# A planner's allowance for transposing DMAs, and the order of loads and distances of attention that go with it

## The chip, the cores and the metric

The kernel runs on one core of a Trainium2 chip. The metric is the device time of one execution in microseconds (us). Names of engines in the profile: PE is TensorE's matrix product (PEld its weight load), DVE is VectorE, ACT is ScalarE, POOL is GpSimd, SP is SyncE, which here only issues DMAs. A transposing DMA copies a tile from SBUF to SBUF and swaps its axes on the way.

## The reference

Chunked attention with a memory, and behind it a gated feed-forward network (FFN) on the same rows:

```python
# q, k, v: (4, 8, 768, 64); mem_k, mem_v: (4, 8, 8, 64); chunk 32, 16 keys left, 8 right
for c in range(24):
    q_c   = q[:, :, 32*c : 32*c+32]
    k_ctx = k[:, :, max(0, 32*c-16) : min(768, 32*c+40)]      # v_ctx alike
    k_full, v_full = concat(mem_k, k_ctx), concat(mem_v, v_ctx)
    a = softmax(q_c @ k_full.T / 8)
    out[:, :, 32*c : 32*c+32] = a @ v_full
x = out.transpose(0, 2, 1, 3).reshape(3072, 512)
gate = maximum(x @ w_gate, 0)          # 512 x 1536
return (gate * (x @ w_val)) @ w_out    # 1536 x 512, float32
```

## The kernel before

**Tiles.** The 3072 rows are 24 attention tiles of 128 rows, `a` = 0 to 23, six to a batch. One tile goes through these steps: transpose queries and keys (`t`), put them where the scores read them (`tc`), scores (`s`, L297), row maximum, subtraction, exponential, sum, reciprocal, normalising (`max`, `sub`, `exp`, `sum`, `rec`, `nrm`), transpose of the normalised weights (`p`, then `pc` if it went through PSUM), product with the values (`v`, L363), copy to the FFN's input (`x`). The FFN works on blocks of 3, 3, 4, 4, 3, 3 and 4 tiles (`BLOCKS`). Block `blk` does twelve times: gate product, value product (`f`, L409), relu on ACT (`r`, L415), multiplication on DVE (`g`, L421). Then come the output products (`o`, L430; four groups of three to a tile), a copy out of PSUM on ACT (`oc`, L91, tile `o_sb`) and a store issued by SP (`os`, L440). `o_sb` has three buffers, the PSUM pool of the FFN (`fps`) has four.

**Who transposes.** Tiles 0 to 5 come as pairs, up to tile 13 (queries) or 14 (keys) tile by tile, and are transposed on PE. From there on (`BY_DMA`, `BY_DMA_P`) queries, keys and weights are transposed by DMAs that SP issues (`qk_dma` L271 with tiles `qT` and `k_t`, `p_dma` L350 with tile `pT`). Keys are then copied from `k_t` to their place by ACT (`tc`, L91 `kT<-k_t`).

**Loads.** POOL issues all loads of queries, keys, values and weights, in the order of the string `LOADS`: `Q0` and `K0` are pairs, `q10` and `k10` single tiles, `v13` a half of batch 0's values (half 1, head pair 3), `z` a memset, `w` a group of FFN columns, `o` a half of `w_out`, `m` the memory's values, `b2` the four loads of batch 2's values. Tiles of queries and keys share 16 buffers.

**Order.** Nothing reorders at run time: each engine runs its list in order. `schedule()` makes the lists by simulating the engines once, when the kernel is built. It gives every step a duration, keeps the time at which each result is there (`done`) and lets a free engine take the ready step with the lowest priority. `LEAD` sets, for each block, how many of the FFN's steps the attention of that block's tiles goes ahead. For a transposing DMA issued by SP (`key[0] in "tpx"`) `done` is the end of the issue plus `BESIDE`, 13 us, or plus `LANDING`, 3 us. Before the change `BESIDE` holds while loads are left to issue, or up to the time at which the queries of the last tile, `("qk", 23, 0)`, are there. In `LOADS` two entries stand behind that tile's `q23` load and others: the last are `k22` and `b3`.

Of the kernel before, what the change touches and what calls it, by code (L numbers as in the profile page):

```python
# [20 lines left out]
def kernel(  # L21
# [24 lines left out]
    NT = B * TPB  # L46
# [3 lines left out]
    CTX = 16 + CH + 8  # L50
    NSET = 2
    BLOCKS = [3, 3, 4, 4, 3, 3, 4]
    LEAD = [24, 10, -1, 2, 7, 6, 14, 22]
    LAST = ((0, 384), (384, 512))
    BY_DMA = (14, 15)
    BY_DMA_P = 14
    LANDING = 3.0
# [1 line left out]
    MEM_BY_SP = 0  # L59
    MEM_LEAD = (0,0,4,4)  # L60
    BY_DMA_X = 24
    BESIDE = 13.0
    LOADS = """Q0 K0 K1 i K2 Q1 Q2 v00 z0 v12 v03 v01 v02 w0 w1 v10 v13 v11 w2 k10
               k8 w3 q6 q7 k7 k6 w4 k9 z2 q9 q8 o1 z1 z3 o0 m b1 k11 q11 q16
               q10 k12 k14 k15 k23 q13 q12 q21 k16 k13 q14 k21 k20 q15 k19 b2 k18 q17 k17 q23
               q18 q22 q19 q20 k22 b3"""

    KEY_RUNS = ((CH, KW, 0), (0, CH, NMEM), (KW, 64, KW))
    assert sum(BLOCKS) == NT and NMEM == 8 and D == 64 and H == 8
# [378 lines left out]
    ops, loads = {}, []  # L448
# [41 lines left out]
    def pace(a):  # L490
        blk = block_of[a]
        if starts[blk] < TPB:
            return []
        m = NDC * (blk - 1) + NDC * (a - starts[blk]) // BLOCKS[blk] - LEAD[blk]
        return [("f", *divmod(max(m, 0), NDC), 0)]
# [4 lines left out]
    for a in range(NT):  # L500
        b, t = divmod(a, TPB)
# [139 lines left out]
    def load_by(name):  # L641
        what, n = name[0], int(name[1:] or 0)
        if what in "qk":
            load_qk_op(n, "qk".index(what))
        elif what in "QK":
            load_pair_op(n, "QK".index(what))
        elif what == "i":
            load("ident", 0, 0.55, lambda: make_identity(nc, ident_h))
        elif what == "v":
            load_v_half(n // 10, [n % 10])  # L650
        elif what == "w":
            load_w_op(n)
        elif what == "z":
            load_zero(n)
        elif what == "m":
            for par in range(2):
                load(("vm", par), 256, 0.3, lambda par=par: mem_values(par))
        elif what == "o":
            load(("wo", n), 768, 4.1, lambda n=n: load_out(n))
        elif what == "b":  # L660
            load_batch(n)

    for name in LOADS.split():
        load_by(name)

    def timed(d):
        return isinstance(d, tuple) and len(d) == 2 and isinstance(d[1], float)
# [8 lines left out]

    def schedule():
        done, started, times = {}, set(), [0.7, 1.25]
        locked = 0.0
        free = {e: 1.25 if e == "POOL" else 0.7 for e in ("PE", "ACT", "DVE", "SP", "POOL")}  # L680
        queue_end, flying, gives = 0.0, [], []
        todo = {e: [] for e in free}
        order, n_load = [], 0
        names = lambda o: [d[0] if timed(d) else d for d in o["deps"]] + o["after"]
        missing = {k: len(set(names(o))) for k, o in ops.items()}
        users = {}
        for k, o in ops.items():
            for d in set(names(o)):
                users.setdefault(d, []).append(k)

        def offer(k):
            for e in ops[k]["eng"]:
                bisect.insort(todo[e], (ops[k]["prio"], k), key=lambda x: x[0])

        for k in ops:
            if not missing[k]:
                offer(k)

        def ready(o, t, margin=0.0):
            if any(d not in started for d in o["after"]):  # L700
                return False
            for d in o["deps"]:
                d, lag = d if timed(d) else (d, 0.0)
                if d not in done or done[d] + lag + margin > t + 1e-9:
                    return False
            return all(room[r] >= o["take"].count(r) for r in o["take"])

        while len(started) < len(ops) + len(loads):
            t = heapq.heappop(times)
            while times and times[0] <= t + 1e-9:  # L710
                heapq.heappop(times)
            for g in [g for g in gives if g[0] <= t + 1e-9]:
                gives.remove(g)
                room[g[1]] += 1
            flying = [f for f in flying if f > t]
            moved = True
            while moved:
                moved = False
                for e in ("POOL", "PE", "ACT", "DVE", "SP"):
                    if free[e] > t + 1e-9:  # L720
                        continue
                    if e == "POOL":
                        if n_load == len(loads):
                            continue
                        o = loads[n_load]
                        if len(flying) >= 8 or not ready(o, t):
                            continue
                        n_load += 1
                        key = o["key"]
                        if o["n"]:  # L730
                            end = t + 0.62 + 0.27e-3 * o["n"]
                            queue_end = max(queue_end, end + 0.8) + o["work"]
                            flying.append(queue_end + 1.0)
                            done[key] = queue_end + (1.2 if n_load < 8 else 2.4 if n_load < 45 else 6.0 if key[0] == "vl" else 4.0)
                        else:
                            end = done[key] = t + o["work"]
                        if locked > t:
                            end += 0.25
                        fn = o["fn"]
                    else:  # L740
                        o = None
                        for _, key in todo[e]:
                            late_pe = e == "PE" and t > 36.0 and ops[key]["prio"][0] == 1
                            if ready(ops[key], t, MARGIN if late_pe else 0.0):
                                o = ops[key]
                                break
                        if o is None and e == "PE" and "ident" in done and 6.0 < t and ("f", 0, 0, 0) not in started:
                            order.append((t, idle_product))
                            free[e] = t + 0.1
                            heapq.heappush(times, free[e])  # L750
                            continue
                        if o is None:
                            continue
                        for x in o["eng"]:
                            todo[x].remove((o["prio"], key))
                        d = o["eng"][e] * (1.8 if e == "PE" and (t < 10.0 and key[0] == "t" or t < 24.0 and key[0] == "p") else 1.0)
                        if e == "DVE" and holds_port(key):
                            end = max(t + d, free["POOL"] + d - 0.1 if free["POOL"] > t else 0.0)
                            locked = end
                        else:  # L760
                            end = t + d
                        done[key] = end + (0.25 if e == "PE" else LAG)
                        if e == "SP" and key[0] in "tpx":
                            done[key] = end + (BESIDE if n_load < len(loads) or t < done["qk", NT - 1, 0] else LANDING)
                        if e == "SP" and key[0] in MOVE:
                            queue_end = max(queue_end, t) + MOVE[key[0]]
                        fn = lambda o=o, e=e: o["fn"](e)
                        for g in o["give"]:
                            g, lag = g if isinstance(g, tuple) else (g, 0.0)
                            gives.append((done[key] + lag, g))  # L770
                            heapq.heappush(times, done[key] + lag)
                    for r in o["take"]:
                        room[r] -= 1
                    started.add(key)
                    for k in users.get(key, ()):
                        missing[k] -= 1
                        if not missing[k]:
                            offer(k)
                    order.append((t, fn))
                    free[e] = end  # L780
                    for x in (end, done[key], done[key] + 0.2, done[key] + 1.5, done[key] + MARGIN):
                        heapq.heappush(times, x)
                    moved = True
            assert times, [k for k in ops if k not in started][:20]
        return order

    for _, fn in schedule():
        fn()
# [30 lines left out]
```

## Time and profile before

| what | value |
|---|---|
| runs | 241.6, 244.89, 245.3 us; median 244.89 us |
| the profiled execution | 243.38 us, of which the span of its instructions is 241.6 us |
| granted TensorE clock | 1.000 |
| busy PE, DVE, ACT, POOL | 225.4, 144.9, 114.9, 92.2 us |
| share of the chain that ended last | PE 60%, DMA 20%, POOL 13% |

The span runs from the first to the last instruction of the trace; the execution's time is 1.78 us longer. Times within the trace count from the span's start. A row of a timeline shows the start of a group of instructions, its length, and in brackets how long the engine had been idle and what ended that. A row of the chain shows start and length of a piece of the sequence of work that ended last. A row of waits shows the total, the number and the longest.

### The profile page before, as it was taken

The numbers are of one execution on the slowest core, as the hardware profiler recorded it, in microseconds if no ns is written. First come the engines' busy times: TensorE is split into PE (matmuls) and PEld (weight loads), VectorE is DVE, ScalarE is ACT, GpSimd is POOL, SyncE is SP. The second block draws the span as 40 slices with busy tenths as digits, with TensorE's granted clock in tenths as the row PEclk, the third lists the DMA queues.
The fourth block names the chain that finished last, engine by engine and source line by source line (L and its number), as shares of the span: only waits on it lengthen the run. The fifth ranks groups of instructions, "written<-read, shape, count | busy, mean of one in ns | idle before, by whom it ended". The sixth has DMA issues, their size and how long they took to land.

```text
span 241.6 us, 5912 instructions
## 1 busy us (share of the span) xinstructions
PE 225.4 (93%) x2446; PEld 125.0 (52%) x2446; DVE 144.9 (60%) x259; ACT 114.9 (48%) x248; POOL 92.2 (38%) x106
## 2 busy tenths in 40 slices
PE   0797989999999999998989799999999999999994
PEld 0676655665544645544434354455556664444442
DVE  4599944569999099775968665059973440234300
ACT  3785753446533855663255452257465441232212
POOL 8999998898648792425700000000000000000000
PEclk9999999999999999999999999999999999999999
DMA  6999999999999999999999962510333001200022
GB/s 72 166 129 137 158 150 175 186 180 175 147 165 207 205 176 96 131 141 120 130 223 163 150 91 27 171 43 3 69 87 111 1 3 43 88 0 0 3 87 87
DMA packets 121115, 27.17 MB, mean 112 GB/s; under 512 B 111232, under 2 KB 118144, under 8 KB 121088
## 3 DMA queue, kind: packets, MB, share of 16 engines
q0 software_dynamic: 101344, 16.61, 95.4%
q1 hardware_dynamic: 19744, 10.18, 21.4%
q8 instruction: 19, 0.31, 0.5%
q14 instruction: 8, 0.07, 0.1%
HBM read 33.24 MB, written 6.29 MB: 164 GB/s over the span
## 4 chain that ended last, share of the span: by engine, by line
PE 60%; DMA 20%; POOL 13%; issue 2%; SPq 2%; DVE 1%; ACT 0%; ACTq 0%; POOLq 0%
PE out_ps L430 19%; PE v_ps L409 19%; PE g_ps L409 18%; DMA qk_b<-in_k_dram 9%; POOL v_bd L187 7%; DMA qk_b<-in_q_dram 4%; DMA pT<-p_n 3%; DMA out_dram<-o_sb 3%; POOL qk_p L218 3%; DMA w_gate_sb<-in_moe_w_gate_dram 2%; SPq L271 2%; PE xT_ps L363 2%; POOL w_gate_sb L118 1%; POOL w_val_sb L118 1%; PE s_ps L297 1%
## 5 line engine op out<-in xcount | busy, mean ns | idle before, releaser
L421 DVE TENSOR_TENSOR gvT<-v_ps,g_relu 128x384 f16<-128x384 f32 (+1 forms) x84 | 51.4, 612 | 57.9 <-PE v_ps L409 47.5
L409 PE MATMUL v_ps<-xT,w_val_sb 128*128 128x384 f16 (+1 forms) x336 | 75.9, 349 | 0.6 <-ACT o_sb L91 0.6
L409 PE MATMUL g_ps<-xT,w_gate_sb 128*128 128x384 f16 (+1 forms) x336 | 75.9, 349 | 0.3 <-DMA w_gate_sb<-in_moe_w_gate_dram 0.3
L415 ACT ACTIVATE g_relu<-g_ps 128x384 f16<-128x384 f32 (+1 forms) x84 | 44.9, 535 | 51.6 <-PE g_ps L409 34.6
L430 PE MATMUL out_ps<-w_out_sb,gvT 128*128 128x512 f16 (+2 forms) x300 | 65.3, 371 | 0.0
L409 PEld LDWEIGHTS <-w_val_sb 128*128 128x128 f16 x336 | 31.6, 98 | 27.1 <-issue 0.9
L409 PEld LDWEIGHTS <-w_gate_sb 128*128 128x128 f16 x336 | 31.6, 98 | 26.6 <-DMA w_gate_sb<-in_moe_w_gate_dram 0.5
L430 PEld LDWEIGHTS <-gvT 128*128 128x128 f16 x300 | 28.0, 98 | 30.3
L91 ACT COPY o_sb<-out_ps 128x512 f32<-128x512 f32 (+2 forms) x25 | 14.2, 567 | 42.8 <-PE out_ps L430 38.3
L187 POOL DMA_DIRECT2D v_bd<-in_v_dram x30 | 30.4, 1034 | 1.1 <-DMA qk_b<-in_q_dram 0.7
L325 ACT ACTIVATE p_exp<-dif 128x64 f16<-128x64 f32 (+2 forms) x72 | 19.6, 338 | 7.4 <-DVE dif L317 7.0
L209 POOL DMA_DIRECT2D qk_b<-in_q_dram x18 | 16.5, 925 | 13.5 <-DMA qT<-qk_b 3.2
L209 POOL DMA_DIRECT2D qk_b<-in_k_dram x18 | 16.9, 952 | 10.6 <-DMA qT<-qk_b 5.1
L329 DVE TENSOR_REDUCE sm<-p_exp 128x8 f32<-128x512 f16 x24 | 16.3, 680 | 2.6 <-ACT p_exp L325 2.4
L310 DVE TENSOR_REDUCE mx<-s_ps 128x8 f32<-128x512 f32 x24 | 16.4, 682 | 1.5 <-PE s_ps L297 1.2
L340 DVE TENSOR_TENSOR p_n<-p_exp,rinv 128x512 f16<-128x512 f16 x24 | 16.5, 687 | 0.5
L163 DVE COPY v_bd<-vmem 8x1536 f16<-8x1536 f16 x24 | 16.6, 722 | 0.2
L317 DVE TENSOR_TENSOR dif<-s_ps,mx 128x512 f32<-128x512 f32 x24 | 16.3, 678 | 0.2
L363 PEld LDWEIGHTS <-v_bd 128*128 128x128 f16 x384 | 12.5, 96 | 6.5 <-issue 2.5
L363 PE MATMUL xT_ps<-pT,v_bd 128*128 128x32 f16 x384 | 12.9, 176 | 2.7 <-DMA pT<-p_n 1.5
L91 ACT CAST xT<-xT_ps 128x512 f16<-128x512 f32 x19 | 10.9, 585 | 9.5 <-PE xT_ps L363 9.5
L401 PE MATMUL idle_ps<-ident_h 128*128 128x128 f16 x101 | 8.4, 227 | 5.4 <-POOL ident_h masks.py:199 5.4
(46 smaller groups left out, 129.2 us busy)
## 6 DMA issues: line engine op xcount, KB each, us to landing
out_dram<-o_sb SPq DMA_DIRECT2D x23, 256.0 KB, 3.0
v_bd<-in_v_dram POOLq DMA_DIRECT2D x11, 336.0 KB, 14.0
qk_b<-in_k_dram POOLq DMA_DIRECT2D x18, 128.0 KB, 8.4
qk_b<-in_q_dram POOLq DMA_DIRECT2D x18, 128.0 KB, 8.6
w_out_sb<-in_moe_w_out_dram POOLq DMA_DIRECT2D x2, 768.0 KB, 8.9
v_bd<-in_v_dram POOLq DMA_DIRECT2D x15, 84.0 KB, 3.9
qk_p<-in_q_dram POOLq DMA_DIRECT2D x3, 256.0 KB, 5.8
qk_p<-in_k_dram POOLq DMA_DIRECT2D x3, 256.0 KB, 5.9
```

Of the source, the lines that this page charges most:

```text
L91: nc.scalar.copy(o, i)
L163: eng.tensor_copy(o, i)
L187: nc.gpsimd.dma_start(dst[64 * par + NMEM + s0:64 * par + NMEM + s1, c0:c1, D * par:D * par + D], bass.AP(tensor=v.tensor, offset=v[b, HP ...
L209: nc.gpsimd.dma_start(qk_b[a, i], bass.AP(tensor=x.tensor, offset=x[b, 0, 128 * t, 0].offset, ap=[[D, 128], [S * D, H], [1, D]]))
L310: nc.vector.reduce_max(SM[a, "mx"], s4, axis=AX.X)
L325: nc.scalar.activation(p[:, :, :, s0:s0 + k1 - k0], dif[:, :, :, k0:k1], ACT.Exp, scale=SCALE)
L340: nc.vector.tensor_tensor(out=P_n[a], in0=SM.pop((a, "p")), in1=rinv_b, op=ALU.mult)
L363: nc.tensor.matmul(ps[:, hp, r], lhsT=v_bd[b % NSET][:, hp, 4 * t + g, :], rhs=x[:, hp, r], start=True, stop=True)
L409: nc.tensor.matmul(ps, lhsT=w[:, f, 128 * m:128 * m + 128], rhs=xTs[blk][:, f, :], start=(f == 0), stop=(f == NFC - 1))
L415: nc.scalar.activation(st["r", m], st.pop((0, m)), ACT.Relu)
L421: nc.vector.tensor_tensor(out=st["gv"][:, m, :], in0=st.pop((1, m)), in1=st.pop(("r", m)), op=ALU.mult)
L430: nc.tensor.matmul(st["o", t, cols], lhsT=st["gv"][:, m, 128 * t:128 * t + 128], rhs=w_out_sb[:, m, slice(*cols)], start=(m == 0), stop=(m ...
```

## The change

The planner notes when the last load lands (`load_end`). A transposing DMA that SP issues before that time is now given `BESIDE`, which goes from 13 to 10 us; after it, `LANDING` as before. `LEAD` and `LOADS` have new values. What is computed and the tiles are the same; the products that PE does while it has nothing else (L401) go from 101 to 94, and some copies change between ACT and DVE.

```diff
-    LEAD = [24, 10, -1, 2, 7, 6, 14, 22]
+    LEAD = [21, 11, -1, 5, 8, 2, 14, 23]
...
-    BESIDE = 13.0
-    LOADS = """Q0 K0 K1 i K2 Q1 Q2 v00 z0 v12 v03 v01 v02 w0 w1 v10 v13 v11 w2 k10
-               k8 w3 q6 q7 k7 k6 w4 k9 z2 q9 q8 o1 z1 z3 o0 m b1 k11 q11 q16
-               q10 k12 k14 k15 k23 q13 q12 q21 k16 k13 q14 k21 k20 q15 k19 b2 k18 q17 k17 q23
-               q18 q22 q19 q20 k22 b3"""
+    BESIDE = 10.0
+    LOADS = """Q0 K0 K1 i Q1 K2 Q2 v00 z0 v02 v03 v01 w0 w1 v13 v11 v12 v10 w2 k8
+               k10 w3 q7 k7 k6 q6 w4 q8 q9 k9 z3 o1 z2 z1 o0 m b1 k11 q16 q10
+               k15 k12 k14 q11 k23 q21 q12 k16 q13 k13 q14 k20 q23 q15 k21 k19 b2 k17 k18 q17
+               q20 q19 q18 q22 k22 b3"""
...
-        locked = 0.0
+        locked = load_end = 0.0
...
-                            flying.append(queue_end + 1.0)
+                            load_end = queue_end + 1.0
+                            flying.append(load_end)
...
-                            done[key] = end + (BESIDE if n_load < len(loads) or t < done["qk", NT - 1, 0] else LANDING)
+                            done[key] = end + (BESIDE if n_load < len(loads) or t < load_end else LANDING)
```

The lists of the engines that come out of it, in the stretch in which block 2's output products end and block 3 begins (names as above; `t17k` is the transposing DMA of tile 17's keys, `o2.1` the output products of block 2's second tile, `f3.0` the gate and value products of block 3's first step, `f3.4g` the gate product alone):

```
SP  before: t14q t15k t15q t16k t16q t18k t17q t17k os2.0 os2.1 os2.2 p14 os2.3 t18q t19k p15 t19q t20k p16
SP  after:  t14q t15k t15q t16k t16q t17k t18k os2.0 t17q os2.1 p14 os2.2 t19k t18q os2.3 p15 t19q t20k p16
ACT before: oc2.0 x13 tc16 oc2.1 exp14 oc2.2 oc2.3 r3.0 exp15 r3.1 r3.2 tc17 r3.3 r3.4 x14 exp16 r3.5 tc18
ACT after:  oc2.0 exp14 x12 x13 tc16 oc2.1 oc2.2 exp15 oc2.3 tc17 r3.0 r3.1 r3.2 exp16 r3.3 r3.4 r3.5 r3.6 x14
PE  before: o2.0 v12 v13 s14 o2.1 ... s15 ... o2.3 f3.0 f3.1 ... f3.4g s16 f3.4v v14 ... f3.6g s17 f3.6v v15 f3.7
PE  after:  ... s14 ... o2.0 o2.1 (1 group) v12 v13 o2.1 ... s15 ... o2.3 f3.0 f3.1 s16 ... f3.6 v14 ... f3.9g v15 f3.9v f3.10g s17
```

On POOL, in the first stage, two loads of `v1x` go from before the weights `w0` and `w1` to behind them; the number of loads ahead of `w2` stays. Ahead of `b2` there is one load more (`q23`). The first of the loads behind `b2` is `k17`; it was `k18`. On PE, `v19` and three of the groups of `o` ahead of block 5's first product change places: it was ahead of eight groups, and is ahead of one group and `s23`.

## The prediction

> **What bounds the kernel now.** I read the page first, then the table of stretches for PE, then PE's waits, and last the chain and the timelines around those waits.
>
> ```profile
> span 241.6 us, 5912 instructions
> PE 225.4 (93%) x2446; PEld 125.0 (52%) x2446; DVE 144.9 (60%) x259; ACT 114.9 (48%) x248; POOL 92.2 (38%) x106
> ...
> L430 PE MATMUL out_ps<-w_out_sb,gvT 128*128 128x512 f16 (+2 forms) x300 | 65.3, 371 | 0.0
> ...
> L401 PE MATMUL idle_ps<-ident_h 128*128 128x128 f16 x101 | 8.4, 227 | 5.4 <-POOL ident_h masks.py:199 5.4
> ```
>
> ```profile
> core 0: us, PE busy (x), PEclk, DMA share, GB/s
> 0.00:34.30 34.30, 24.11 (x542) 1.00 1.51 135
> 34.30:107.00 72.70, 72.68 (x776) 1.00 2.00 165
> 107.00:137.00 30.00, 27.30 (x307) 1.00 2.08 157
> 137.00:238.40 101.40, 101.26 (x825) 1.00 0.23 55
> 238.40:241.60 3.20, 0.00 (x0) 1.00 0.24 82
> ```
>
> From 34.3 to 238.4 us PE has work all the time, except for 2.70 us (30.00 - 27.30) between 107 and 137. The clock is full everywhere. So three things can move the end: the first 34.3 us, those 2.70 us, and any new hole. The 3.2 us behind the last product are the last copies and stores, which the change leaves alone.
>
> The 2.70 us are three waits, in brackets in PE's timeline:
>
> ```profile
> 110.93 0.77 PE L363 MATMUL xT_ps<-pT,v_bd 128*128 128x32 f16 x24 [0.60 <-DMA v_bd<-in_v_dram]
> ...
> 123.38 1.02 PE L409 MATMUL v_ps<-xT,w_val_sb 128*128 128x512 f16 x4 [0.63 <-ACT o_sb L91]
> ...
> 135.59 0.55 PE L363 MATMUL xT_ps<-pT,v_bd 128*128 128x32 f16 x16 [1.47 <-DMA pT<-p_n]
> ```
>
> I call them A (0.60, batch 2's values), B (0.63, the copy `oc2.3`) and C (1.47, the transposing DMA of tile 15's weights). The chain tells where B and C begin:
>
> ```profile
> 90.18 21.38 DMA qk_b<-in_k_dram
> ...
> 111.58 1.25 SPq L271
> ...
> 112.93 1.68 SPq L271
> ...
> 114.70 1.27 SPq L271
> ...
> 116.07 6.58 DMA out_dram<-o_sb
> ...
> 122.74 0.59 ACT o_sb L91
> ...
> 127.42 8.13 DMA pT<-p_n
> ```
>
> ```profile
> 122.74 0.58 ACT L91 COPY o_sb<-out_ps 128x512 f32<-128x512 f32 x1 [4.55 <-DMA out_dram<-o_sb]
> ...
> 123.71 0.81 ACT L325 ACTIVATE p_exp<-dif 128x64 f16<-128x64 f32 x3
> ```
>
> SP stands until tile 18's keys are loaded (111.56), issues three transposing DMAs, and only then the store `os2.0`. That store lands 6.58 us later; its buffer is the one `oc2.3` needs, so ACT stands 4.55 us. That is B. Behind `oc2.3` on ACT stand `r3.0` and tile 15's exponentials (123.71), so its normalised weights come late, the DMA is issued at 127.42 and lands 8.13 us later. That is C: mostly late issue, then a landing for which the old plan had allowed 3 us (all loads were issued).
>
> **The change part by part.** *The allowance.* How long do such DMAs take? First the stretch with loads in flight (111 to 137), then the one without (140 to 200):
>
> ```profile
> k_t<-qk_b SPq DMA_TRANSPOSE x5, 6.5
> qT<-qk_b SPq DMA_TRANSPOSE x4, 8.1
> pT<-p_n SPq DMA_TRANSPOSE x3, 6.9
> ...
> pT<-p_n SPq DMA_TRANSPOSE x7, 2.4
> ```
>
> Beside loads 6.5 to 8.1 us at the median, alone 2.4: ten from the issue's end covers it, three did not. On SP's and ACT's lists this shows as follows. Tile 15's exponentials now stand ahead of `oc2.3`, no longer behind a store. `p15` follows `os2.3`: `oc2.3` ends about 122.5 (next paragraph), so `p15` goes out near 123.1 instead of 127.42, 4.3 us earlier. `v15` stands five products of block 3 later, behind `f3.9g` instead of `f3.6v`: 5 x 0.86 = 4.3 us, from this row of the chain.
>
> ```profile
> 141.33 0.86 PE g_ps L409 x4
> ```
>
> Together 8.6 us against a wait of 1.47: C goes, with 7.1 us of cover. *C: -1.47; bounds -1.47 and 0.* `v14` moves back four products in the same way and does not get tight.
>
> A page of the Trainium skill would have it otherwise. "DMA: Bandwidth & Descriptors", section "Anatomy of one DMA — SWDGE (gpsimd) path", fits about 2.0 us plus the bytes over 436e3 to one DMA, stated for GpSimd's queue; for this tile of 128 KB that is an estimate of 2.3 us. By it the old 3 us were right, ten could take nothing off C, and the sum would be 243.38 - 0.63 + 0.3 = 243.1. The trace agrees only where no load flies (2.4), not beside loads (6.5 to 8.1), so the measurement decides.
>
> *The store.* The first load behind `b2` is now `k17`, one load later than `k18` was, since `q23` comes ahead of `b2`. POOL's row for such an issue:
>
> ```profile
> 90.18 0.92 POOL L209 DMA_DIRECT2D qk_b<-in_k_dram  x1
> ```
>
> So the keys land near 111.56 + 0.92 = 112.5. Two transposing DMAs instead of three then stand ahead of `os2.0`: before, 116.07 - 111.58 = 4.49 us, without the `qT` one (114.70 - 112.93 = 1.77) 2.72. It goes out at 115.2, lands 6.58 later at 121.8, and `oc2.3` ends 0.1 + 0.59 later, at 122.5. PE wants the buffer at 123.38 - 0.63 = 122.75. *B: -0.63; bounds -0.63 and 0,* as the cover is only 0.25.
>
> *Batch 2's values.* `b2` is one load later (+0.92). Ahead of `v12` PE now has one group of output products more (65.3 / 300 x 3 = 0.65) and `s14` (0.24 in the row below): 0.89.
>
> ```profile
> 55.03 0.24 PE s_ps L297 x32
> ```
>
> *A: stays 0.60; bounds -0.60 (gone) and +0.92 (no cover for the load).*
>
> *The first stage.* Two loads of the values' second half go behind `w0` and `w1`, and `Q1` ahead of `K2`. Seven idle products of 8.4 / 101 = 0.083 fall away, so block 0's first product can start 0.58 us earlier. But what ends this stage comes later:
>
> ```profile
> 32.29 0.85 PE L363 MATMUL xT_ps<-pT,v_bd 128*128 128x32 f16 x28 [0.36 <-DMA v_bd<-in_v_dram]
> 33.42 0.55 PE L363 MATMUL xT_ps<-pT,v_bd 128*128 128x32 f16 x16 [0.27 <-ACT xT L91]
> 34.32 1.48 PE L409 MATMUL g_ps<-xT,w_gate_sb 128*128 128x384 f16 x8 [0.35 <-DMA w_gate_sb<-in_moe_w_gate_dram]
> ```
>
> At 32.3 PE waits for the last of those loads, at 34.3 for `w2`, and as many loads stand ahead of both as before. The 0.58 us become a longer wait ahead of 32.3. *0; bounds -0.58 and 0.* If these loads came sooner, the gain would be real.
>
> *A new place for `tc17`.* ACT copies tile 17's keys right behind `oc2.3`, ahead of `r3.0`, and `s16` follows `f3.1v`. PE reaches `s16` at 122.75 + 0.86 = 123.6; less 0.61 for the copy and 0.1 for hand-overs, the DMA must land by 122.9. Issued at 112.5 it has 10.4 us; the row for `k_t` from 80 to 140 is:
>
> ```profile
> DMA to landing us min/median/max: 5.2/8.1/10.8
> ```
>
> *0; bounds 0 and 0.4.* Behind a late `tc17` stand all relus of block 3, and behind them PE.
>
> *Block 5's input.* `v19` moves from eight groups ahead of block 5 to one group and `s23`. From `v19` to the end of `x19`'s copy takes 136.18 - 135.59 + 0.58 = 1.17 and a hand-over of 0.1; its cover is 0.40 + 0.65 + 0.24 = 1.29.
>
> ```profile
> 136.18 0.58 ACT L91 CAST xT<-xT_ps 128x512 f16<-128x512 f32 x1 [2.57 <-PE xT_ps L363]
> ```
>
> One `o_sb` copy (0.59) in its way would show in full: *0 to 0.59*. For this and for B's thin cover I take half, *+0.3*.
>
> **Sum,** against the profiled execution's own time, 241.6 + 1.78 = 243.38: -1.47 - 0.63 + 0.3 = -1.8, so **241.6 us**. The three runs shown are 241.6 to 245.3 with a median of 244.89: 1.5 above the profiled one, 1.3% above the forecast. A spread of 3.7 us fits waits whose length hangs on when DMAs land, which the new lists bind less. The limit of 2% is about what a measurement of this kernel can tell from no change: below 240.0 or above 249.8.
>
> **The rivals.** *More than forecast.* A goes as well, and the first stage keeps its 0.58: 243.38 - 2.70 - 0.58 = 240.1. For it: the values' loads in question go out at the same rate and the weights sooner. Against it: `b2` comes later, and the rows at 32.3 and 34.3 wait for POOL's list.
>
> *The waits only move.* A grows by what B and C give back, or `p15` is late for another reason (DVE is 60% busy): 243.4. For it: A's load is later and B's cover 0.25. Against it: C's 7.1 us of cover. The page named above leads to nearly this time, 243.1, with C alone left.
>
> *Slower: `tc17` waits.* If tile 17's keys land as late as loads do in that stretch, ACT and then PE stand. From a landing after 122.9 + 1.8 = 124.7, 12.2 us behind the issue, the gain is eaten. With 19.1 us, the median of batch 2's loads, it lands at 131.6 and the time is 241.6 + 8.7 = 250.3.
>
> ```profile
> v_bd<-in_v_dram POOLq DMA_DIRECT2D x4, 336.0 KB, 19.1
> ```
>
> For it: this DMA meets `b3`'s loads. Against it: of the rows above none took over 10.8 us.
>
> **How the numbers follow.** Forecast 0.58 (own range 240.7 to 242.8), more 0.13, waits move 0.19, slower 0.10. Over 2% faster are the lower part of "more" and some luck of the runs: 0.11. Over 2% slower: most of the last case, 0.07. The rest, 0.82, is within 2%. The range goes from 240.0, the first rival, to 245.0, the present median, and leaves out the slow case.
>
> **What would show it.** Right: in the stretch 107 to 137 PE is idle under 1 us; no wait of PE for `pT` or `o_sb`; ACT's exponentials of tile 15 ahead of `oc2.3`; `k_t` of tile 17 down before 122.9; A still there; PE's first product near 25.4 but w2's still near 34.3. Wrong: a PE wait for `k_t` or ACT near 123, a wait ahead of block 5 near 180, or a first stage that ends before 33.8.

## The result and the profile after

The kernel after takes 240.74 us (median of 22 runs, 239.74 to 242.62) against 243.68 us before on the same chip (22 runs, 241.37 to 246.94). The ratio is 0.9916, interval 0.989 to 0.9943: 0.8% faster, inside the 2%. The ratios leave out runs that lie over 1.5% above the fastest of their kernel, so the medians of all runs, given here and below, can lie further apart (here 240.74/243.68 = 0.988). A second measurement among the experiments gave 0.9917 (0.9893 to 0.9941). The profiled execution took 240.34 us against 243.38, its span 238.6 against 241.6.

From the page of the kernel after:

```profile
span 238.6 us, 5900 instructions
PE 225.6 (95%) x2439; PEld 125.1 (52%) x2439; DVE 142.6 (60%) x258; ACT 116.3 (49%) x249; POOL 92.3 (39%) x106
...
PE 85%; POOL 11%; DMA 2%; issue 1%; ACT 0%; ACTq 0%; POOLq 0%
```

PE is as long busy as before (225.6 against 225.4 us) in a span 3.0 us shorter. In the chain that ended last DMAs have fallen from 20% to 2%: from the first product of block 1 to the last product nothing but PE itself is on it. The table of stretches for PE says where the 3 us were (from, to, length, busy):

```profile
34.30:107.00 72.70, 72.69 (x782) 1.00 1.98 165
107.00:137.00 30.00, 30.00 (x292) 1.00 1.98 159
137.00:235.40 98.40, 98.24 (x844) 1.00 0.22 55
```

Between 107 and 137 us PE was idle for 2.70 us and now is not idle at all. All three waits are gone, A too. PE's timeline at the three places, none of them with a bracket (`v12`; the value product of `f3.1`, which had waited for `oc2.3`; `v15`), and what stands ahead of the last:

```profile
111.11 0.95 PE L363 MATMUL xT_ps<-pT,v_bd 128*128 128x32 f16 x32
...
121.97 1.03 PE L409 MATMUL v_ps<-xT,w_val_sb 128*128 128x512 f16 x4
...
135.67 1.03 PE L409 MATMUL g_ps<-xT,w_gate_sb 128*128 128x512 f16 x4
136.53 0.56 PE L363 MATMUL xT_ps<-pT,v_bd 128*128 128x32 f16 x16
```

SP's timeline shows when the transposing DMA `p15` (at 122.34) and the store `os2.0` (at 112.10) go out; the row under it, from the tile `pT` between 108 and 140 us, how long the DMAs took from issue to landing:

```profile
109.49 2.52 SPq L271 DMA_TRANSPOSE k_t<-qk_b  x2
112.10 0.92 SPq L440 DMA_DIRECT2D out_dram<-o_sb  x1
...
122.34 1.23 SPq L350 DMA_TRANSPOSE pT<-p_n  x1
...
DMA to landing us min/median/max: 7.1/7.5/7.9
```

The row on landings is of `p15`'s neighbours: `p14` took 7.1 us and `p16` 7.9; the trace has no landing for `p15` itself. It went out at 122.34 and PE asked for it at 136.53, 14.19 us later, and did not wait. With 7.9 us it was there at 130.24 (an estimate), 6.3 us before that. ACT's timeline has tile 15's exponentials (118.71) ahead of `oc2.3` (120.84), and `tc17` right behind it without a wait:

```profile
118.71 0.81 ACT L325 ACTIVATE p_exp<-dif 128x64 f16<-128x64 f32 x3 [1.14 <-DVE dif L317]
120.84 0.58 ACT L91 COPY o_sb<-out_ps 128x512 f32<-128x512 f32 x1 [1.31 <-DMA out_dram<-o_sb]
121.32 0.62 ACT L91 COPY kT<-k_t 128x512 bf16<-128x512 bf16 x1
```

The first stage is as long as before: the products of block 0 begin at 26.13 us (26.03 before), block 1's second group at 35.78 (35.63).

```profile
26.13 0.81 PE L409 MATMUL g_ps<-xT,w_gate_sb 128*128 128x384 f16 x4
...
32.61 1.03 PE L363 MATMUL xT_ps<-pT,v_bd 128*128 128x32 f16 x32 [0.40 <-DMA v_bd<-in_v_dram]
...
34.31 1.64 PE L409 MATMUL g_ps<-xT,w_gate_sb 128*128 128x384 f16 x8
35.78 0.81 PE L409 MATMUL v_ps<-xT,w_val_sb 128*128 128x384 f16 x4
```

**What a wait costs.** Three idle times of 2.70 us and a first stage 0.15 later make 2.55, but the span fell by 3.0. The rows of the products say why: the one at 135.67 is 1.03 long, and the next starts 0.86 after it. The end of a product in the trace is modelled, 0.16 to 0.17 behind the start of the next. An idle time is counted from that modelled end, so each wait costs about 0.16 more than its bracket says: 2.70 + 3 x 0.16 - 0.15 = 3.03.

### The profile page after: what moved, and what is told of

The parts are those of the page before. It is cut to its first block, busy times and chain, and to the rows that moved or that the text cites. A ratio compares the mean times of both kernels' runs of the same rounds, so it can differ in the third digit from the quotient of the medians.

```text
span 238.6 us, 5900 instructions
## 1 busy us (share of the span) xinstructions
PE 225.6 (95%) x2439; PEld 125.1 (52%) x2439; DVE 142.6 (60%) x258; ACT 116.3 (49%) x249; POOL 92.3 (39%) x106
## 3 DMA queue, kind: packets, MB, share of 16 engines
q1 hardware_dynamic: 19744, 10.18, 20.4%
## 4 chain that ended last, share of the span: by engine, by line
PE 85%; POOL 11%; DMA 2%; issue 1%; ACT 0%; ACTq 0%; POOLq 0%
PE out_ps L430 26%; PE v_ps L409 25%; PE g_ps L409 25%; POOL v_bd L187 5%; PE xT_ps L363 3%; POOL qk_p L218 3%; DMA v_bd<-in_v_dram 2%; PE s_ps L297 2%; PE qk_ps L262 2%; POOL w_gate_sb L118 1%; POOL w_val_sb L118 1%; PE pT_ps L346 1%; POOL v_bd L132 1%; POOL ident_h masks.py:197 0%; ACT xT L91 0%
## 5 line engine op out<-in xcount | busy, mean ns | idle before, releaser
L310 DVE TENSOR_REDUCE mx<-s_ps 128x8 f32<-128x512 f32 x24 | 16.4, 682 | 2.5 <-PE s_ps L297 2.2
L401 PE MATMUL idle_ps<-ident_h 128*128 128x128 f16 x94 | 8.2, 230 | 5.4 <-POOL ident_h masks.py:199 5.4
```

The lines of the kernel that those rows point to most:

```text
L310: nc.vector.reduce_max(SM[a, "mx"], s4, axis=AX.X)
```

## The experiments

The theory going in: C is what limits the kernel, and the allowance cures it. Tile 15's weights are issued some 5 us too close to the product that reads them, because the old plan let the transposing DMA land after 3 us. Rivals: the searched lists (`LEAD`, `LOADS`) bring the gain; the store's buffer is the root, since B and C lie on one chain; the first stage has a share.

**The rule alone**

```diff
-    BESIDE = 13.0
+    BESIDE = 10.0
...
-        locked = 0.0
+        locked = load_end = 0.0
...
-                            flying.append(queue_end + 1.0)
+                            load_end = queue_end + 1.0
+                            flying.append(load_end)
...
-                            done[key] = end + (BESIDE if n_load < len(loads) or t < done["qk", NT - 1, 0] else LANDING)
+                            done[key] = end + (BESIDE if n_load < len(loads) or t < load_end else LANDING)
```

> The kernel before with only the planner's new rule (ten us up to the landing of the last load); LEAD and LOADS as before. Theory 1, the three waits were three causes: the rule moves tile 15's exponentials ahead of oc2.3 and v15 three products later, so C (the wait for pT) goes; os2.0 still stands behind three transposing DMAs, so B stays, and b2 keeps its place, so A stays. PE idle between 107 and 137 falls from 2.70 to about 1.2 us, the time by 1.5 to 1.6 us, ratio about 0.993. Rival, the new lists carry the gain: ratio 1.000, C still there.

240.85 us (240.04 to 242.96), ratio 0.9929 (0.9889 to 0.9969): nearly all of it. The table of stretches for PE:

```profile
107.00:140.00 33.00, 33.00 (x336) 1.00 2.06 152
```

No wait is left with the old lists either. The expectation had kept A and B, 1.2 us in all, and was wrong there. `v12` stands behind `s14` and later in this plan (111.03 us, 109.97 before). That B is gone as well hangs on the loads: the first of the three transposing DMAs ahead of the store went out at 110.35 us, not at 111.58, and `oc2.3` ended 0.6 us before PE took up its product.

**The lists alone**

```diff
-    LEAD = [24, 10, -1, 2, 7, 6, 14, 22]
+    LEAD = [21, 11, -1, 5, 8, 2, 14, 23]
...
-    LOADS = """Q0 K0 K1 i K2 Q1 Q2 v00 z0 v12 v03 v01 v02 w0 w1 v10 v13 v11 w2 k10
...
+    LOADS = """Q0 K0 K1 i Q1 K2 Q2 v00 z0 v02 v03 v01 w0 w1 v13 v11 v12 v10 w2 k8
...
```

> The kernel before with only the new LEAD and LOADS; the rule and 13 us as before. Theory 1: os2.0 stands behind two transposing DMAs, so B goes (0.63, 0.79 with the refill of PE's pipeline); v12 stands later, so A goes; exponentials of tile 15 still stand behind oc2.3 and r3.0, so C stays, 0.8 to 1.6 us. Ratio about 0.994 to 0.996. Rival, the rule carries the gain: ratio 1.000. Rival, the lists carry all of it: ratio 0.990 and no wait of PE between 107 and 137.

243.18 us (240.92 to 245.91), ratio 1.0022 (0.9977 to 1.0068). PE's timeline, and `p15` in the chain:

```profile
130.47 0.55 PE L363 MATMUL xT_ps<-pT,v_bd 128*128 128x32 f16 x16 [0.63 <-DMA pT<-p_n]
...
134.99 0.55 PE L363 MATMUL xT_ps<-pT,v_bd 128*128 128x32 f16 x16 [0.51 <-DMA pT<-p_n]
...
125.86 9.08 DMA pT<-p_n
```

Now `v14` and `v15` both wait. The lists bring nothing by themselves: the ratio is not the 0.994 to 0.996 that was expected.

**A buffer of its own for `oc2.3`** (the kernel before, B taken away at its root; the buffer is one of the first stage that is free by then)

```diff
-        o = opool.tile([128, cols[1] - cols[0]], F32, name="o_sb")
+        if (blk, t) == (2, 3):
+            o = prpool.tile([128, cols[1] - cols[0]], F32, tag="qk_p", name="o_sb")
+        else:
+            o = opool.tile([128, cols[1] - cols[0]], F32, name="o_sb")
```

> The kernel before, all lists the same, but the output tile of block 2's fourth tile (oc2.3) lies in a buffer of the first stage that is long free, so that oc2.3 doesn't wait for the store os2.0. Theory 1 (B and C are one chain that begins at that store): ACT's 4.5 us wait goes, B goes, the exponentials of tile 15 start near 121.5 instead of 123.7, p15 goes out near 125 instead of 127.4 and C goes or is under 0.5 us: 2.0 to 2.4 us less, ratio about 0.990 to 0.992. Rival (C is the landing beside loads, for which 3 us were too few): only B goes, 0.6 to 0.8 us, ratio 0.997, C over 1 us.

242.15 us (240.78 to 244.92), ratio 0.9977 (0.9944 to 1.001). ACT's timeline (`oc2.3`, then tile 15's exponentials), the chain, PE's timeline:

```profile
120.18 0.58 ACT L91 COPY o_sb<-out_ps 128x512 f32<-128x512 f32 x1 [2.00 <-PE out_ps L430]
...
121.60 0.80 ACT L325 ACTIVATE p_exp<-dif 128x64 f16<-128x64 f32 x3
...
125.43 8.74 DMA pT<-p_n
...
134.21 0.55 PE L363 MATMUL xT_ps<-pT,v_bd 128*128 128x32 f16 x16 [0.89 <-DMA pT<-p_n]
```

B is gone, ACT's 4.55 us are gone, `p15` goes out 2.0 us sooner (125.43 against 127.42), and C falls only to 0.89, between the two expectations. PE asks 0.80 us sooner (133.32 against 134.12), and the landing took 8.74 instead of 8.13: -1.99 + 0.61 + 0.80 = -0.58. The store has a share in C, but that it is the root of C, as the prediction's chain had it, falls: an issue 2 us earlier did not make up for a plan that had allowed 3 us for a landing of 8.7.

**The first line of `LOADS` alone** (in the kernel before)

```diff
-    LOADS = """Q0 K0 K1 i K2 Q1 Q2 v00 z0 v12 v03 v01 v02 w0 w1 v10 v13 v11 w2 k10
+    LOADS = """Q0 K0 K1 i Q1 K2 Q2 v00 z0 v02 v03 v01 w0 w1 v13 v11 v12 v10 w2 k10
```

> The kernel before with only the first line of the new LOADS, up to w2. Theory: the first stage ends with w2 and the last of the values' second halves, ahead of which as many loads stand as before, so f0.4 starts at 34.3 as before and the ratio is 1.000 (0.997 to 1.003). Rival: the 0.6 us by which block 0 could start earlier are kept, ratio 0.9975, or the later values cost some tenths, ratio 1.001 to 1.002.

245.04 us (242.13 to 247.61), ratio 1.0056 (1.0012 to 1.01), a little slower. Its first stage ends as the others do (`f1.0v` at 36.02). The chain and PE's table:

```profile
126.37 10.09 DMA pT<-p_n
...
137.05 1.71 PE g_ps L409 x4
...
107.00:140.00 33.00, 29.58 (x312) 0.95 2.14 149
```

`p15` landed 10.09 us after its issue and C was 3.42 us (33.00 - 29.58). The granted clock of 0.95 in that stretch comes from the time right behind this wait: from 136.5 to 141 us it was 0.62, before and after 1.00, and the three products there took 4.27 us from start to start instead of 3 x 0.86, 1.69 us more. So C cost far more here than its bracket. Behind the wait of 2.99 us in the next experiment the product took its usual 1.02 us; that the length of the wait brings the lower clock is not shown by one profile. Whether the new first line makes the landing later or this was its usual spread, one profile can't say either; the last experiment takes it up.

**Ten alone** (the kernel before, old rule, only the number)

```diff
-    BESIDE = 13.0
+    BESIDE = 10.0
```

> The kernel before with BESIDE 10 instead of 13 and nothing else: old rule, old lists. By the old rule tile 15's transposing DMA still counts as landed 3 us after its issue. The planner now also puts tile 15's exponentials ahead of oc2.3, so p15 goes out about 122.4 (as after), but v15 stands right behind f3.4v, which PE reaches near 128.8 (f3.0 starts near 119.4, ten products of 0.86, v14 0.41, s16 0.24). Landings took 7.1 to 10.1 us beside loads. Theory 1 (what counts is that the place of v15 leaves room for the landing): p15 lands at 129.5 to 132, PE waits 0.7 to 3 us for pT, ratio to before 0.998 to 1.005. Rival (what counts is the order on ACT, exponentials ahead of the copy that waits for a store, so that the number 10 carries the gain): no wait for pT, ratio 0.993.

244.48 us (241.39 to 247.1), ratio 1.0029 (0.9978 to 1.008). SP's timeline, chain and PE's timeline:

```profile
123.15 1.32 SPq L350 DMA_TRANSPOSE pT<-p_n  x1
...
123.15 9.50 DMA pT<-p_n
...
122.75 1.02 PE L409 MATMUL v_ps<-xT,w_val_sb 128*128 128x512 f16 x4 [0.37 <-ACT o_sb L91]
...
132.69 0.55 PE L363 MATMUL xT_ps<-pT,v_bd 128*128 128x32 f16 x16 [2.99 <-DMA pT<-p_n]
```

The clearest of the runs. Tile 15's exponentials are early here, as after, and `p15` goes out 4.3 us sooner than before (123.15 against 127.42). But the planner, which still gave it 3 us, moved `v15` forward as well: PE asks at 132.69 - 2.99 = 129.70, before at 134.12, 4.4 us later. With a landing of 9.50 C grew to 2.99. An early issue is worth what the place of the reader leaves of it.

**Six instead of ten** (the kernel after)

```diff
-    BESIDE = 10.0
+    BESIDE = 6.0
```

> The kernel after with BESIDE 6 instead of 10: new rule, new lists. v14 stands behind f3.2v, v15 behind f3.4v, two and a half us earlier than what landings of 7.1 to 10.1 us allow if p15 goes out at 121 to 122.4. Theory 1: PE waits for pT at v15 (0.5 to 2.5 us), perhaps also at v14; ratio to before 0.995 to 1.001. Rival (the order on ACT carries the gain; the allowance beyond 6 is not needed): no wait for pT of 0.3 us or more, ratio 0.992 as after.

242.22 us (240.61 to 245.74), ratio 0.9956 (0.992 to 0.9991), between the two kernels. SP's and PE's timelines:

```profile
120.96 1.24 SPq L350 DMA_TRANSPOSE pT<-p_n  x1
...
130.13 0.57 PE L363 MATMUL xT_ps<-pT,v_bd 128*128 128x32 f16 x16 [0.83 <-DMA pT<-p_n]
```

Six is too short: `p15` goes out 1.4 us sooner than after, but PE asks 7.2 us sooner (130.13 - 0.83 = 129.30 against 136.53) and stands 0.83 us, since the landing took 9.1 us.

**Thirteen with the new rule** (the kernel after)

```diff
-    BESIDE = 10.0
+    BESIDE = 13.0
```

> The kernel after with BESIDE 13 instead of 10: new rule, new lists, the old number. p15 stands behind os2.3, p14 and two transposing DMAs; v14 goes behind f3.10v, v15 into the output products of block 3. Theory 1 (any allowance above the landings will do; from 10 to 13 only spare time grows): PE waits for nothing between 107 and 137, ratio to before 0.992, the same as after within the interval. Rival (the smaller number is part of the gain: with 13 the products of the attention come so late that block 4's input or the exponentials become late): a new wait of PE, ratio 0.996 or more.

240.78 us (240.34 to 244.29), ratio 0.9931 (0.9899 to 0.9964). SP's timeline, PE's timeline (`v15`), the table of stretches:

```profile
125.84 1.19 SPq L350 DMA_TRANSPOSE pT<-p_n  x1
...
143.57 0.56 PE L363 MATMUL xT_ps<-pT,v_bd 128*128 128x32 f16 x16
...
107.00:140.00 33.00, 33.00 (x322) 1.00 1.67 139
```

The same as ten: spare time above the landing costs nothing here. So what counts in the change is the condition, that the allowance now reaches tile 15, not its new number. The cleanest pair for this is the run with the lists alone, which differs from this one in the condition only. There `p15` went out at 125.86 us, here at 125.84. What moved is the reader: PE asked for it at 134.48 (134.99 - 0.51) there and waited, and at 143.57 here and did not.

**A memset behind the weights** (the kernel after; `z0` of 1.4 us moves from behind `v00` to behind `w2`; the lists of all other engines are the same)

```diff
-    LOADS = """Q0 K0 K1 i Q1 K2 Q2 v00 z0 v02 v03 v01 w0 w1 v13 v11 v12 v10 w2 k8
+    LOADS = """Q0 K0 K1 i Q1 K2 Q2 v00 v02 v03 v01 w0 w1 v13 v11 v12 v10 w2 z0 k8
```

> The kernel after with one memset of POOL (z0, 1.4 us by the planner's time, zeroes of the second buffer of the values) moved from ahead of the sixth load of values to behind w2; the lists of all other engines are the same. It tells what bounds the first stage. Theory 1 (POOL's issue of the loads ends the stage): w2 is issued up to 1.4 us earlier, PE's wait for v_bd near 32 and for w2 near 34.3 shrink, the first product of block 1 starts up to 1.0 us earlier, ratio to before down to 0.988. Rival (the DMA engines are the bound, or the end of the stage is set by the exponentials behind the loads): the loads are issued earlier and land at the same time, span within 0.2 us of after, ratio 0.992.

240.55 us (239.53 to 243.24), ratio 0.9887 (0.9828 to 0.9946). PE's timeline:

```profile
33.41 1.64 PE L409 MATMUL g_ps<-xT,w_gate_sb 128*128 128x384 f16 x8
...
121.92 1.02 PE L409 MATMUL v_ps<-xT,w_val_sb 128*128 128x512 f16 x4 [0.69 <-ACT o_sb L91]
```

POOL's list does set the end of the first stage: block 1 begins 0.90 us sooner. In this profile B gave the gain back, 0.69 + 0.16 = 0.85 us, and the span was 238.5. PE now reaches `oc2.3`'s buffer sooner than the store frees it; the store also went out 1.16 us later than in the kernel after (113.26 against 112.10).

**The same memset in the kernel before**

```diff
-    LOADS = """Q0 K0 K1 i K2 Q1 Q2 v00 z0 v12 v03 v01 v02 w0 w1 v10 v13 v11 w2 k10
+    LOADS = """Q0 K0 K1 i K2 Q1 Q2 v00 v12 v03 v01 v02 w0 w1 v10 v13 v11 w2 z0 k10
```

> The kernel before with the same memset z0 moved behind w2 (as in the last run of the kernel after, where block 1 began 0.90 us earlier); all other lists as before. Theory 1 (before, the end is set by fixed times behind the loads: the store os2.0 and the landing of tile 15's weights; PE that comes sooner only waits longer): block 1's first product starts near 33.4 instead of 34.3, the PE waits between 107 and 140 grow together by about 0.9 us, span within 0.4 us of before, ratio 0.998 to 1.002. Rival (gains add: the first stage and the waits are independent): span 0.9 us shorter, ratio 0.996.

242.92 us (239.87 to 245.77), ratio 0.9961 (0.9917 to 1.0005), inconclusive between the two. PE's timeline:

```profile
27.18 0.81 PE L409 MATMUL g_ps<-xT,w_gate_sb 128*128 128x384 f16 x4
...
34.55 1.64 PE L409 MATMUL g_ps<-xT,w_gate_sb 128*128 128x384 f16 x8
...
134.38 0.55 PE L363 MATMUL xT_ps<-pT,v_bd 128*128 128x32 f16 x16 [1.43 <-DMA pT<-p_n]
```

In this profile block 0's first product began 1.15 us later than before (27.18 against 26.03), so that its stage ended no sooner, and the test of what the waits do with a shorter stage did not take place in it. C is there (1.43), B and A are not.

**Memset and buffer together** (the kernel after with both edits above)

> The kernel after with the memset z0 behind w2 and, besides, oc2.3 copied into a free buffer of the first stage, so that this copy waits for no store. Theory 1: block 1 begins near 33.4, B (0.69 us with the memset alone) is gone, the only wait that can come instead is A (batch 2's values landed between 106.8 and 110.9, PE now reaches v12 near 109.3): span 237.5 to 238.0 without A, ratio to before 0.985 to 0.989. Rival (the tail behind the last product or another store takes over): span 238.5 as with the memset alone, ratio 0.989 to 0.992.

239.76 us in the median of six runs that lie between 239.51 and 240.03; ratio 0.9869 (0.9838 to 0.99). PE's timeline and table:

```profile
33.48 1.63 PE L409 MATMUL g_ps<-xT,w_gate_sb 128*128 128x384 f16 x8
...
107.00:140.00 33.00, 33.00 (x336) 1.00 1.81 148
```

The first stage keeps its 0.83 us and B does not come back: span 237.7. This is the version that beats both kernels: its median lies 1.06 us under that of the kernel after (0.4%; 240.82 on the same chip), and its slowest run, 240.03, is under the fastest of the kernel after there, 240.22.

**The kernel after again**

> The kernel after itself, unchanged, on the same chip as the other runs of this call, for comparison and for the spread of its landings. All theories: ratio to before 0.989 to 0.994, span 238.4 to 239.2, no wait of PE for pT; the wait for batch 2's values (A) present or not by when b2 lands (106.8 to 110.9 so far, 110.2 is where PE asks).

240.82 us (240.22 to 242.75), ratio 0.9917 (0.9893 to 0.9941), span 238.6, no wait of PE between block 1 and the last product.

**The kernel after with the old first line of `LOADS`**

```diff
-    LOADS = """Q0 K0 K1 i Q1 K2 Q2 v00 z0 v02 v03 v01 w0 w1 v13 v11 v12 v10 w2 k8
+    LOADS = """Q0 K0 K1 i K2 Q1 Q2 v00 z0 v12 v03 v01 v02 w0 w1 v10 v13 v11 w2 k8
```

> The kernel after with the old first line of LOADS, so that the first stage is the one of before. Theory 1 (the order of the values' loads in the first stage is worth nothing; the 1.0056 of the new first line in the kernel before came from C): ratio the same as after within the interval, block 1's products f1.0v start at 35.6 to 36.4. Rival (the new first line costs up to 0.5 per cent): this one is faster than after by 0.3 to 0.5 per cent.

240.68 us (240.59 to 241.09), ratio 0.991 (0.9878 to 0.9941), the same as after (0.9917). The order of the values' loads is worth nothing that shows; the 1.0056 of the new first line in the old plan is not a longer first stage (`f1.0v` at 36.02 there, 36.16 here). That it came from C is argued from one profile, not shown.

**All spans in one sum.** Take from each profile where block 1's second group `f1.0v` starts and the brackets of PE's waits behind it, and put 238.6 + (f1.0v - 35.78) + each wait + 0.16:

| kernel | f1.0v | waits behind it | sum | span |
|---|---|---|---|---|
| before | 35.63 | A 0.60, B 0.63, C 1.47 | 241.6 | 241.6 |
| rule alone | 36.34 | none | 239.2 | 239.2 |
| lists alone | 36.24 | `v14` 0.63, C 0.51 | 240.5 | 240.5 |
| buffer | 36.38 | C 0.89 | 240.3 | 240.2 |
| ten alone | 36.02 | B 0.37, C 2.99 | 242.5 | 242.5 |
| six | 36.16 | C 0.83 | 240.0 | 240.0 |
| thirteen | 36.22 | none | 239.0 | 239.0 |
| memset | 34.88 | B 0.69 | 238.5 | 238.5 |
| memset, old plan | 36.02 | C 1.43 | 240.4 | 240.4 |
| memset and buffer | 34.95 | none | 237.8 | 237.7 |
| after again | 35.82 | none | 238.6 | 238.6 |
| old first line | 36.16 | none | 239.0 | 239.0 |

Every span comes out within 0.1 us: beside the first stage and these waits nothing moves the end. The profile of the first line alone is not in the table; with the 1.69 us of slow products it comes to 238.6 + 0.24 + 3.42 + 0.16 + 1.69 = 244.1, for a span of 244.2. With the old rule C is there in all six profiles (0.51 to 3.42 us); with the new rule and ten or more, in none of seven.

## Why the prediction was right, and where it was not

The forecast was 241.6 us and a change within 2%, the result 240.74 us and a ratio of 0.9916. Against its own execution it had -1.8 us; the spans say -3.03. The difference of 1.23 is A (0.60), the hidden part of three waits (0.48) and the +0.3 that was not needed, less a first stage 0.15 later. The stated range, 240.0 to 245.0, was wide: it also holds the 244.89 of no change and the 243.4 of "the waits only move" (and 244.89 is 1.4%, not 1.3%, above the forecast). That the time lies in it says little; the waits that went say more.

**C, -1.47: right, with a larger price.** The cause was the landing, for which the old plan left too little time: 8.1 to 10.1 us for `p15` with the old rule; in the two profiles of the kernel after, its neighbours took 7.1 to 9.6. `p15` was forecast out at 123.1 and went out at 122.34. The cover was to be 7.1; it is about 6 with the 8.13 us that the sum had used, and 4.1 with the slowest landing, 10.09. The price was 1.47 + 0.16. One link failed: the prediction had the chain run from the loads over the store and `oc2.3` to C, "mostly late issue". With the buffer of its own the issue came 2.0 us sooner and C fell only to 0.89; with ten alone it came 4.3 us sooner and C doubled. A reader that moves back with the allowance is enough, as the lists alone and the run with thirteen show with the same time of issue. Whether an issue 5 us sooner would do with the reader left in its place, no run tests; in the kernel after both moved.

The estimate of 2.3 us for such a DMA, worked out in the prediction from the Trainium skill, "DMA: Bandwidth & Descriptors", section "Anatomy of one DMA — SWDGE (gpsimd) path", and the time of 243.1 that followed from it, do not hold beside loads: the trace disagrees, as tile 15's DMA took 8.1 to 10.1 us there, and with an allowance of 6 PE still waited 0.83 us. The measurement decides.

**B, -0.63: right in size, for a thin reason.** The keys came down at 109.49, not 112.5, so that `os2.0` went out at 112.10, not 115.2. Most of that was spent again, since the store took 8.6 us to free the buffer (112.10 to 120.74, a hand-over of 0.1 ahead of 120.84), not 6.58: `oc2.3` ended at 121.42 and PE took up its product at 121.97, a cover of about 0.5 against the 0.25 forecast. That the loads came early is luck: with the old rule and the same order of these loads, the first of SP's transposing DMAs here went out at 111.58 (before), 109.93 (ten alone), 109.04 (first line alone) and 108.60 (memset, old plan), and B was 0.63, 0.37 and twice nothing. The +0.3 for B and block 5's input was not needed in any profile of the kernel after; with a stage 0.9 us shorter B did come back at 0.69.

**A, kept at 0.60: wrong.** The bounds held it (-0.60 was one end), the choice did not. In none of the thirteen other profiles, with old lists or new, does PE wait for batch 2's values. The slowest of these loads took 22.1 us in the profile of before and 16.4 to 20.4 in the others: one profiled execution had a late load, and the prediction took it for a property of the order.

**The first stage, 0: right.** Block 1's first product began at 34.31 against 34.32. That it agrees so closely is luck: its second group, `f1.0v`, began at 35.63 to 36.38 us in the profiles with the old first line and at 35.78 to 36.24 with the new, the moved memset apart. The term 0 holds within that spread, though the first product did not begin at 25.4 as the prediction's check had it but at 26.13: the seven idle products less did not move it. That as many loads ahead of `w2` mean the same end was the right reason: with 1.4 us less on POOL's list ahead of them the stage ended 0.83 and 0.90 us sooner than in the kernel after; in the old plan's profile it did not. (The two loads that moved behind `w0` and `w1` are the two DMAs of one entry of `LOADS`, `v12`.)

**`tc17`, 0: right.** Its DMA went out at 109.49 and ACT copied at 121.32 without a wait. The slow rival had no part.

**The rivals.** "More than forecast" (240.1) was nearest in time: A did go. But the first stage kept nothing, and A went by itself. "The waits only move" fell for the kernel after and holds in part for single cures: without B, C was still 0.89; with a shorter stage, B was 0.69.

## What to carry to other kernels

Give a planner the latency that a transfer has in the company it keeps, and check the condition that switches between two latencies first: here the tile that hurt was on the wrong side of it, and its number (10 or 13) did not matter as long as it was above the measured landing. Where waits stand in a row, removing an early one or issuing sooner mostly feeds the next; move the reader, and look at the next place that PE will reach sooner. Read which waits recur over several executions before pricing them, and add to each the part that the modelled end of a product hides.

## What the runs showed of the hardware

- The transposing DMA of tile 15's weights took 8.1 to 10.1 us from issue to landing beside loads in the six profiles with the old rule, 2.4 being the median without loads. The spread of C (0.51 to 3.42 us) that comes with it would account for much of the spread of the kernel before (241.4 to 246.9 us), but C is known only where a profile was taken, so this is argued. The kernel after spreads from 239.7 to 242.6, the version with memset and buffer from 239.5 to 240.0.
- The same list of loads came down up to 3.8 us apart from run to run (SP's first transposing DMA of the stretch at 107.75 in the run with the buffer, at 111.58 before).
- Block 0's first product began anywhere from 25.77 to 27.18 us with nearly the same lists ahead of it. What moves it was not found.
- Behind PE's longest wait after the first stage, 3.42 us, the granted clock was 0.62 for 4.5 us and products took up to twice their time (1.71 us from start to start, 0.86 else), which cost 1.69 us more. One profile (first line alone) shows it; behind the waits there of up to 2.99 us no profile does.
